# Spreading the loads of a fused attention and gMLP kernel between its compute, and moving the copies of V next to their use

## The chip, the cores and the metric

One core of one Trainium2 chip. The metric is the device time of one execution in microseconds (us), the median of several. Five engines matter: PE (matmuls; PEld is its weight load), DVE (vector), ACT (activation), POOL (here it issues the loads, and does some small arithmetic), and SP, which issues the stores. Each engine works through its own queue of instructions in order, as the stall shown below makes visible for DVE. The granted clock is the share of its full clock that PE was allowed to run at, as the profile records it. All executions quoted here are fast: none was more than 1.5% slower than the fastest of the same kernel.

## The reference

Eight batches of 576 positions, eight heads of 64. Heads 0 to 3 attend to the last 32 positions ("plain"), heads 4 to 7 to every fourth of the last 128 ("dilated"). The result is x of a gated MLP whose gate mixes positions with the 576 x 576 matrix w_sg.

```python
attn = softmax(where(mask, q @ k.T / 8, -1e9)) @ v        # per batch and head
x    = attn as [8, 576, 512]
h    = gelu(x @ w_in);  u, v2 = halves of h
v_n  = (v2 - mean) / sqrt(var + 1e-6) * g_ln              # over the 512 columns
out  = x + (u * (w_sg @ v_n + b_sg)) @ w_out
```

## The kernel before

The kernel runs ten periods p. In period p the attention of batch p is done, z and u of batch p-1, and the gate and output of batch p-2. Each period has two halves: transposes T and scores S with gate and output, then AV and the transposes X with z and u. Operations stay in program order on each engine. The parts that the change touches:

```python
def load(b, step):                       # all loads of a batch, issued by POOL
    ...                                  # q, k, v of the plain heads, q, k of the dilated
    x = v[b][4:8].rearrange("h (m r) d -> m h (r d)", r=4)
    dma(vm.rearrange("p h r d -> p h (r d)"), x[0:KB])
    for r in range(2):
        dma(vt[r:KB:2]..., x[NM - 64:NM, :, D * r:D * r + 3 * D])
    nc.vector.tensor_copy(vd[:, :, 0:4, 0:D], vm)                  # DVE, waits for vm
    nc.vector.tensor_copy(vd[:, :, 4:6, 0:D], vt[:, :, 0:3:2, :])  # DVE, waits for vt

def a_T(b, g):                           # q and k transposed by PE, then copied
    ...
    nc.scalar.copy(k0, pk[0:64, :, 0:HS])            # ACT
    nc.vector.tensor_copy(k1, pk[64:128, :, 0:HS])   # DVE: needed before the scores

setup_consts(); load(0, 2); load_weights(); load(1, 4)
for p in range(B + 2):
    merge(T and S of p, gate and output of p - 2)    # period 0: also prep_wsg
    merge(AV and X of p, z and u of p - 1)
    if p + 2 < B:
        load(p + 2, 4)                   # behind all compute of the period
```

The masks of heads 3 and 7, and the two small operations rs (a power of the variance), are done by POOL, in the same queue as the load issues.

The softmax here doesn't subtract the row's maximum and nothing guards it: scores larger than these inputs give would overflow.

## Time and profile before

| | before |
|---|---|
| median | 417.7 us |
| busy: PE / DVE / ACT / POOL | 61% / 46% / 44% / 34% |
| length of periods 2 to 6 | 47.4 to 48.9 us |
| DVE idle ahead of the vm copies | 127.6 us over 8 copies |
| granted PE clock, whole span | 0.88 |

No engine is near full. These are the engine line of the profile page, and its strip of 40 slices of about 10.5 us: a digit is the busy share in tenths, or the granted clock in tenths.

```profile
PE 256.0 (61%) x2494; PEld 180.3 (43%) x2494; DVE 191.5 (46%) x378; ACT 183.2 (44%) x270; POOL 140.3 (34%) x193
...
PE   1010285198518972598808974378807978889994
...
DVE  7000472248035560638317380556407386486280
...
PEclk9999999998958987598956988599865999989999
```

DVE drops to 0 or near it again and again, and the clock digit of PE drops to 5 or 6 about as often. The list of waits says who waited for whom (total us, times, longest):

```profile
DVE vd_90 L151 <- DMA vm<-in_v_dram: 72.4, 4, 24.7
DVE vd_89 L151 <- DMA vm<-in_v_dram: 55.2, 4, 15.4
```

Its PE part shows the wait that follows from that one:

```profile
PE pss L214 <- DVE kT_1_83 L205: 24.1, 2, 12.7
PE pss L214 <- DVE kT_1_79 L205: 22.8, 2, 11.6
PE pss L214 <- DVE kT_1_81 L205: 22.7, 2, 12.0
PE pw L167 <- DMA wsg_73<-in_moe_w_sg_dram: 21.2, 1, 21.2
...
PE pxt L270 <- DVE onorm L254: 16.6, 12, 2.1
```

The timeline shows one such stall (start, duration, engine, line, operation; in brackets the idle time before it and what ended it):

```profile
150.44 3.14 POOL L121 DMA_DIRECT2D qp<-in_q_dram  x4
...
152.57 0.96 DVE L254 TENSOR_TENSOR onorm<-poa,rc 128x768 f16<-128x768 f32 x1
...
156.13 1.39 PE L336 MATMUL pv<-wsgT_74,vn 128*128 128x288 f16 x10 [0.15 <-ACT xT L279]
...
160.74 1.30 POOL L121 DMA_DIRECT2D vt<-in_v_dram  x2
168.91 0.43 DVE L151 COPY vd_89<-vm 128x1024 f16<-128x1024 f16 x1 [15.37 <-DMA vm<-in_v_dram]
170.04 0.29 DVE L152 COPY vd_89<-vt 128x512 f16<-128x512 f16 x1 [0.71 <-DMA vt<-in_v_dram]
170.37 0.76 DVE L205 CAST kT_1_79<-pk 64x576 f16<-64x576 f32 x1
...
171.18 0.64 PE L214 MATMUL pss<-qT,kT_0_78 128*128 128x96 f16 x6 [11.24 <-DVE kT_1_79 L205]
...
173.31 2.56 PE L336 MATMUL pv<-wsgT_74,vn 128*128 128x288 f16 x10 [0.64 <-DVE kT_1_81 L205]
```

POOL starts to issue the loads only when period 2's compute has left its queue, at 150.4, and needs until 162.0. The last of them lands at 170.0. DVE finished its work of the period at 153.5, but the next thing in its queue is the copy of vm, which belongs to batch 4 and will not be read before the second half of period 4. Behind it stands the kT copy that period 3's scores need at once. Thus DVE waits 15.4 us, and PE 11.2 us. Ten L336 matmuls take 1.39 us before the stall and 2.56 us after it.

### The profile page before, as it was taken

What the parts mean: (1) busy time and instruction counts of PE and PEld (TensorE: products, weight loads), DVE (VectorE), ACT (ScalarE), POOL (GpSimd) and SP (SyncE); (2) the same over time, 40 slices, a digit from 0 to 9 for tenths busy, and PEclk for the clock granted to TensorE, in tenths of its full rate; (3) what the DMA queues carried; (4) which work ended last, traced back from release to release, by engine and by line L of the source; (5) the groups of instructions that cost most, each with busy time, mean ns of one, the idle gap of its engine ahead of it and who ended that gap; (6) DMA issues with size and microseconds to landing.
All of it is one profiled execution on the core that took longest, in us unless ns stands there. A gap on an engine that the chain in (4) does not pass through costs nothing.

```text
span 418.0 us, 6143 instructions
## 1 busy us (share of the span) xinstructions
PE 256.0 (61%) x2494; PEld 180.3 (43%) x2494; DVE 191.5 (46%) x378; ACT 183.2 (44%) x270; POOL 140.3 (34%) x193
## 2 busy tenths in 40 slices
PE   1010285198518972598808974378807978889994
PEld 0010184165415551454605653255605557556462
DVE  7000472248035560638317380556407386486280
ACT  2000076074613853256803755157713768564422
POOL 8736039025801275013911167013920220130030
PEclk9999999998958987598956988599865999989999
DMA  9999509701960369111990339411990300110303
GB/s 129 140 205 115 73 2 103 94 2 7 106 83 0 114 45 134 17 54 62 82 112 2 115 20 121 55 52 63 63 133 3 114 2 2 72 44 0 114 0 113
DMA packets 91467, 28.91 MB, mean 69 GB/s; under 512 B 71664, under 2 KB 86064, under 8 KB 91440
## 3 DMA queue, kind: packets, MB, share of 16 engines
q0 software_dynamic: 85232, 18.47, 49.9%
q1 hardware_dynamic: 6208, 10.06, 7.0%
q8 instruction: 19, 0.31, 0.3%
q14 instruction: 8, 0.07, 0.0%
HBM read 37.53 MB, written 9.44 MB: 112 GB/s over the span
## 4 chain that ended last, share of the span: by engine, by line
PE 22%; DVE 22%; DMA 19%; POOL 18%; ACT 12%; issue 6%; POOLq 0%; ACTq 0%; DVEq 0%
DMA vt<-in_v_dram 14%; PE po L353 6%; DVE st L303 5%; PE pv L336 5%; DMA w_out_72<-in_moe_w_out_dram 4%; POOL kp L121 4%; DVE vs L340 3%; PE pu L323 3%; POOL qp L121 3%; ACT osb L359 3%; DVE gat L343 2%; DVE onorm L254 2%; ACT vv L298 2%; PE po L356 2%; POOL vp_88 L121 2%
## 5 line engine op out<-in xcount | busy, mean ns | idle before, releaser
L336 PE MATMUL pv<-wsgT_74,vn 128*128 128x288 f16 x320 | 52.2, 320 | 8.6 <-ACT qT L196 2.9
L196 ACT CAST qT<-pq 128x576 f16<-128x576 f32 x32 | 20.6, 644 | 65.2 <-PE pq L185 49.6
L353 PE MATMUL po<-w_out_72,gat 128*128 128x512 f16 x160 | 42.7, 379 | 10.4 <-DVE gat L343 8.5
L323 PE MATMUL pu<-xT,w_in_71 128*128 128x288 f16 x256 | 43.8, 326 | 2.0 <-ACT xT L279 1.9
L336 PEld LDWEIGHTS <-vn 128*128 128x128 f16 x320 | 34.4, 108 | 22.3 <-issue 9.9
L294 PE MATMUL pz<-w_in_71,xT 128*128 128x512 f16 x160 | 39.0, 394 | 0.0
L359 ACT COPY osb<-po 128x1024 f32<-128x1024 f32 (+1 forms) x24 | 21.0, 875 | 39.9 <-PE po L356 32.5
L303 DVE BATCH_NORM_STATS2 st<-vv 128x6 f32<-128x512 f32 x40 | 26.9, 673 | 21.5 <-ACT vv L298 21.4
L151 DVE COPY vd_90<-vm 128x1024 f16<-128x1024 f16 x4 | 1.7, 429 | 72.4 <-DMA vm<-in_v_dram 72.4
L323 PEld LDWEIGHTS <-w_in_71 128*128 128x128 f16 x256 | 26.7, 110 | 11.1 <-issue 2.5
L254 DVE TENSOR_TENSOR onorm<-poa,rc 96x768 f16<-96x768 f32 (+1 forms) x32 | 30.6, 955 | 1.1
L340 DVE SCALAR_TENSOR_TENSOR vs<-pv,g_col,b_bc 128x576 f16<-128x576 f32 x32 | 26.1, 816 | 8.7 <-PE pv L336 8.1
L326 ACT ACTIVATE u<-pu 128x576 f16<-128x576 f32 x32 | 22.2, 693 | 17.5 <-PE pu L323 17.5
L151 DVE COPY vd_89<-vm 128x1024 f16<-128x1024 f16 x4 | 1.7, 429 | 55.2 <-DMA vm<-in_v_dram 55.2
L167 PE MATMUL pw<-ident_69,wsg_73 96*128 96x96 f16 x30 | 2.9, 277 | 39.2 <-DMA wsg_73<-in_moe_w_sg_dram 21.2
L121 POOL DMA_DIRECT2D qp<-in_q_dram x32 | 25.3, 797 | 3.7 <-DMA kd<-in_k_dram 2.0
L121 POOL DMA_DIRECT2D kp<-in_k_dram x32 | 23.1, 735 | 9.2 <-DMA w_in_71<-in_moe_w_in_dram 4.3
L305 POOL TENSOR_SCALAR rs<-mv 128x2 f32<-128x2 f32 (+1 forms) x24 | 5.8, 240 | 60.2 <-DVE mv L304 60.2
L270 PE MATMUL pxt<-ident_69,onorm 96*128 96x96 f16 (+2 forms) x192 | 15.3, 221 | 16.8 <-DVE onorm L254 16.6
L298 ACT ACTIVATE vv<-pz 128x1024 f32<-128x1024 f32 (+1 forms) x24 | 21.0, 881 | 8.6 <-PE pz L294 7.8
L353 PEld LDWEIGHTS <-gat 128*128 128x128 f16 x160 | 14.0, 97 | 23.7 <-DVE gat L343 13.0
L294 PEld LDWEIGHTS <-xT 128*128 128x128 f16 x160 | 15.3, 102 | 16.9 <-issue 2.7
(179 smaller groups left out, 552.4 us busy)
## 6 DMA issues: line engine op xcount, KB each, us to landing
out_dram<-osb SPq DMA_DIRECT2D x32, 256.0 KB, 2.2
qp<-in_q_dram POOLq DMA_DIRECT2D x32, 72.0 KB, 3.0
kp<-in_k_dram POOLq DMA_DIRECT2D x32, 72.0 KB, 3.1
qd<-in_q_dram POOLq DMA_DIRECT2D x8, 288.0 KB, 7.5
kd<-in_k_dram POOLq DMA_DIRECT2D x8, 288.0 KB, 8.5
vm<-in_v_dram POOLq DMA_DIRECT2D x8, 256.0 KB, 8.8
vt<-in_v_dram POOLq DMA_DIRECT2D x16, 96.0 KB, 8.6
vp_88<-in_v_dram POOLq DMA_DIRECT2D x4, 288.0 KB, 6.0
```

What stands on the lines that cost most here:

```text
L121: nc.gpsimd.dma_start(dst, src)
L196: nc.scalar.copy(qT, pq[:, :, 0:HS])
L254: nc.vector.tensor_tensor(onorm.rearrange("p a h d -> p h a d"), pv[:, :, :, 0:64], rc.unsqueeze(3).broadcast_to([rows, 2, NB, 64]), AO.mult)
L294: nc.tensor.matmul(pz[:, c, :], xT[:, g4, MT[ti]:MT[ti] + 128], w_in16[:, g4, DH:DFF], start=(g4 == 0), stop=(g4 == 3))
L298: nc.scalar.activation(vv[:, 0:n], pz[:, 0:n], AF.Gelu_apprx_tanh)
L303: nc.vector.bn_stats(st[:, c, :], vv[:, c, :])
L323: nc.tensor.matmul(pu[:, j, 0:HS], w_in16[:, g4, 128 * ph:128 * ph + 128], xT[:, g4, HS * j:HS * j + HS], start=(g4 == 0), stop=(g4 == 3))
L326: nc.scalar.activation(us[b][:, ph, :].rearrange("p (j w) -> p j w", j=2), pu[:, :, 0:HS], AF.Gelu_apprx_tanh)
L336: nc.tensor.matmul(pv[:, j, 0:HS], vn[:, kp, 128 * ph:128 * ph + 128], wsgT16[:, kp, HS * j:HS * j + HS], start=(kp == 0), stop=(kp == 4))
L340: nc.vector.scalar_tensor_tensor(vs.rearrange("p (j w) -> p j w", j=2), pv[:, :, 0:HS], g_col[:, ph:ph + 1], b_bc.rearrange("p (j w) -> p ...
L353: nc.tensor.matmul(po[:, c, :], gat[:, ph, ts], w_out16[:, ph, :], start=(ph == 0), stop=False)
L359: nc.scalar.copy(osb[:, 0:n], po[:, 0:n])
```

## The change

Its intent: get the loads off the critical path, by splitting a batch's loads into pieces, putting the pieces between compute one to two periods ahead of use, moving the vd copies to the period that reads them, and moving the w_sg transposes from period 0 to 1. A new merge rule comes with it, for three lists in place of two. The core of the diff (comments stand for what is cut):

```diff
-        nc.vector.tensor_copy(vd[:, :, 0:4, 0:D], vm)              # inside load(b)
-        nc.vector.tensor_copy(vd[:, :, 4:6, 0:D], vt[:, :, 0:3:2, :])
+    def cp_vd(b):                                   # now a piece of its own
+        vm, vt = vraw.pop(b)
+        vd = vds[b % NV]
+        nc.vector.tensor_copy(vd[:, :, 0:4, 0:D], vm)
+        nc.vector.tensor_copy(vd[:, :, 4:6, 0:D], vt[:, :, 0:3:2, :])
...
-    def merge(one, other):                          # i1 * n2 <= i2 * n1 decides whose turn it is
+    def merge(*lists):
+        items = [((i + 0.5) / len(x), n, i, f) for n, x in enumerate(lists)
+                 for i, f in enumerate(x)]
+        for _, _, _, (f, *a) in sorted(items, key=lambda t: t[:3]):
+            f(*a)
...
-    load(0, 2); load_weights(); load(1, 4)
+    # batch 0 and w_in here; batch 1 inside period 0, w_sg at its end, w_out in period 1
     for p in range(B + 2):
-                   (a_S, p, 6), (a_S, p, 7)]
-        if p == 0:
-            mlp = [(prep_wsg,)]
+                   (a_S, p, 6), (a_S, p, 7), (cp_vd, p)]
+        if p == 1:
+            mlp = [(prep_wsg, i) for i in range(5)]
+        # first half:  io = [(ld_vp, p + 1, 0, 4), (ld_vd, p + 1)]
+        # second half: io = [(ld_plain, p + 2, 0), (ld_plain, p + 2, 2), (ld_dil, p + 2)]
-        if p + 2 < B:
-            load(p + 2, 4)
```

More of the change, by code (lines that the diff above doesn't have):

```diff
@@ L117, in setup_consts @@
             nc.vector.memset(t[:, S:PTW], 1.0)
+        nc.vector.memset(wsgT16[0:64, 4, :], 0.0)
     def dma(dst, src):
@@ L123, with open_batch @@
     loaded = {}
-    def load(b, step):
+    def open_batch(b):
         qp = ld.tile([QB, NB, 4, D], FP16, tag="qp", name="qp")
@@ L129, in load, with ld_plain, ld_dil, ld_vp @@
         kd = ld.tile([TB, 4, 2, 4, D], FP16, tag="kd", name="kd")
+        loaded[b] = ((qp, kp), (qd, kd))
+    def ld_plain(b, h0):
+        if h0 == 0:
+            open_batch(b)
+        for t, src in zip(loaded[b][0], (q, k)):
+            for h in range(h0, h0 + 2):
+                dma(t[:, :, h, :], src[b][h].rearrange("(a p) d -> p a d", p=QB))
+    def ld_dil(b):
+        for t, src in zip(loaded[b][1], (q, k)):
+            dma(t.rearrange("p h f r d -> p (h f) (r d)"),
+                src[b][4:8].rearrange("h (f p r) d -> p (h f) (r d)", p=TB, r=4))
+    def ld_vp(b, h0, n):
+        vp = vps[b % NV]
+        x = v[b][h0:h0 + n].rearrange("h (a p) d -> p (h a) d", p=QB)
+        y = vp[:, h0:h0 + n].rearrange("p h a d -> p (h a) d")
+        dma(y[HALO:KB, :, 0:D], x)
+        dma(y[0:HALO, 1:, 0:D], x[QB - HALO:QB, 0:n * NB - 1])
+    vraw = {}
+    def ld_vd(b):
         vm = ld.tile([KB, 4, 4, D], FP16, tag="vm", name="vm")
         vt = ld.tile([KB, 4, 3, D], FP16, tag="vt", name="vt")
-        vp, vd = vps[b % NV], vds[b % NV]
-        loaded[b] = ((qp, kp), (qd, kd), vp, vd)
-        for h0 in range(0, 4, step):
-            hs = slice(h0, h0 + step)
-            for t, src in ((qp, q), (kp, k)):
-                for h in range(h0, h0 + step):
-                    dma(t[:, :, h, :], src[b][h].rearrange("(a p) d -> p a d", p=QB))
-            x = v[b][hs].rearrange("h (a p) d -> p (h a) d", p=QB)
-            y = vp[:, hs].rearrange("p h a d -> p (h a) d")
-            dma(y[HALO:KB, :, 0:D], x)
-            dma(y[0:HALO, 1:, 0:D], x[QB - HALO:QB, 0:step * NB - 1])
-        for t, src in ((qd, q), (kd, k)):
-            dma(t.rearrange("p h f r d -> p (h f) (r d)"),
-                src[b][4:8].rearrange("h (f p r) d -> p (h f) (r d)", p=TB, r=4))
         x = v[b][4:8].rearrange("h (m r) d -> m h (r d)", r=4)
@@ L150, in load, with ld_win, ld_wsg @@
                 x[NM - 64:NM, :, D * r:D * r + 3 * D])
+        vraw[b] = (vm, vt)
+    def cp_vd(b):
+        vm, vt = vraw.pop(b)
+        vd = vds[b % NV]
         nc.vector.tensor_copy(vd[:, :, 0:4, 0:D], vm)
         nc.vector.tensor_copy(vd[:, :, 4:6, 0:D], vt[:, :, 0:3:2, :])
-    def load_weights():
+    def ld_win():
         dma(w_in16, moe_w_in.rearrange("(g p) f -> p g f", p=128))
+    def ld_wsg():
+        dma(wsg16, moe_w_sg.rearrange("(a p) s -> p a s", p=QB))
         nc.sync.dma_start(b_bc, moe_b_sg.unsqueeze(0).to_broadcast([128, S]))
@@ L158, in load_weights, with ld_wout, prep_wsg @@
             nc.sync.dma_start(g_col, moe_g_ln.rearrange("(c p) -> p c", p=128))
-        dma(wsg16, moe_w_sg.rearrange("(a p) s -> p a s", p=QB))
+    def ld_wout():
         dma(w_out16, moe_w_out.rearrange("(g p) f -> p g f", p=128))
-    def prep_wsg():
-        nc.vector.memset(wsgT16[0:64, 4, :], 0.0)
-        for kp in range(5):
-            pw = psum("pw")
-            for a in range(NB):
-                nc.tensor.matmul(
-                    pw[:, a // 3, QB * (a % 3):QB * (a % 3) + QB],
-                    wsg16[:, a, MT[kp]:MT[kp] + 128], ident16[0:QB, 0:QB],
-                    start=True, stop=True)
-            lo = 64 if kp == 4 else 0
-            nc.vector.tensor_copy(
-                wsgT16[lo:128, kp, :].rearrange("p (j w) -> p j w", j=2),
-                pw[lo:128, :, 0:HS])
+    def prep_wsg(kp):
+        pw = psum("pw")
+        for a in range(NB):
+            nc.tensor.matmul(
+                pw[:, a // 3, QB * (a % 3):QB * (a % 3) + QB],
+                wsg16[:, a, MT[kp]:MT[kp] + 128], ident16[0:QB, 0:QB],
+                start=True, stop=True)
+        lo = 64 if kp == 4 else 0
+        nc.vector.tensor_copy(
+            wsgT16[lo:128, kp, :].rearrange("p (j w) -> p j w", j=2),
+            pw[lo:128, :, 0:HS])
     qkT, PTs, onorms, xTs = {}, {}, {}, {}
     def a_T(b, g):
-        plain, dil, _, _ = loaded[b]
+        plain, dil = loaded[b]
         pq, pk = psum("pq"), psum("pk")
@@ L234, in a_AV @@
     def a_AV(b, g):
-        _, _, vp, vd = loaded[b]
+        vp, vd = vps[b % NV], vds[b % NV]
         poa = psum("poa")
@@ L362, in m_out @@
             nc.sync.dma_start(out[b][MT[ti] + lo:MT[ti] + 128, :], osb[lo:128, c, :])
-    def merge(one, other):
-        n1, n2 = len(one), len(other)
-        i1 = i2 = 0
-        while i1 < n1 or i2 < n2:
-            if i2 >= n2 or (i1 < n1 and i1 * n2 <= i2 * n1):
-                f, *a = one[i1]
-                i1 += 1
-            else:
-                f, *a = other[i2]
-                i2 += 1
+    def merge(*lists):
+        items = [((i + 0.5) / len(x), n, i, f) for n, x in enumerate(lists)
+                 for i, f in enumerate(x)]
+        for _, _, _, (f, *a) in sorted(items, key=lambda t: t[:3]):
             f(*a)
     setup_consts()
-    load(0, 2)
-    load_weights()
-    load(1, 4)
+    for h0 in (0, 2):
+        ld_plain(0, h0)
+    ld_vp(0, 0, 4)
+    ld_dil(0)
+    ld_vd(0)
+    ld_win()
     for p in range(B + 2):
-        att, mlp = [], []
+        att, mlp, io = [], [], []
         if p < B:
@@ L393 @@
                    [(m_out, p - 2, i) for i in range(3)])
-        merge(att, mlp)
-        att, mlp = [], []
+        if p + 1 < B:
+            if p == 0:
+                io = [(ld_plain, 1, 0), (ld_plain, 1, 2), (ld_dil, 1)]
+            io += [(ld_vp, p + 1, 0, 4), (ld_vd, p + 1)]
+        if p == 0:
+            io += [(ld_wsg,)]
+        if p == 1:
+            io += [(ld_wout,)]
+        merge(att, mlp, io)
+        att, mlp, io = [], [], []
         if p < B:
@@ L402 @@
             mlp += [(m_zu, p - 1, ph) for ph in range(1, 4)]
-        merge(att, mlp)
         if p + 2 < B:
-            load(p + 2, 4)
+            io = [(ld_plain, p + 2, 0), (ld_plain, p + 2, 2), (ld_dil, p + 2)]
+        merge(att, mlp, io)
 _INS = ['q', 'k', 'v', 'moe_w_in', 'moe_g_ln', 'moe_w_sg', 'moe_b_sg', 'moe_w_out']
```

## The prediction

> **What bounds the kernel now.** No engine is full: the page's busy shares are PE 61%, DVE 46%, ACT 44%, POOL 34%. The loads bound it. In the chain of waits "DMA vt<-in_v_dram" alone holds 14% of the span. The mechanism, from the timeline of one period: the loads of batch p+2 are queued on POOL after all compute of period p; POOL issues them from 150.4 to 162.0 us, the last landing at 170.0. The two vd copies stand in DVE's in-order queue ahead of the next period's first kT copy, so DVE sits idle 15.4 us (list of waits: 72.4 + 55.2 us over 8 such copies), and PE, needing kT, idles 11.2 us. This repeats six times at a period of 48.2 us, and batch 1 delays period 0 in the same way (24.7 us).
>
> A second cost follows: after each idle stretch PE is slow. The windows view gives granted clock 0.50 to 0.62 in the first 7.8 us, and ten L336 matmuls take 2.5 us there, 1.39 us elsewhere. The Trainium skill, "TensorE: Matmul & The Clock Gate" (Part 1), says that an idle window of about 3.4 us halves the clock until sustained work restores it; the trace agrees.
>
> **What the change does.** It removes no work. Copies of vd move to the end of the first half of the period that uses them, a period after their loads were issued; loads are issued between compute, a period or more before use. Added on POOL: nothing, but its 15 load issues (about 0.8 us each, 12 us a period) now stand between the masks and the rs operations, which can be late by up to 3 us. w_sg's transposes (PE 2.9, DVE 3.5 us) move from period 0 to 1. The new merge order should fill PE gaps of 2.1 (before X1) and 1.8 us (before the output).
>
> **Size.** Period 7 in the present trace has no load stall either before or after it: PE runs from 346.5 to 380.7, 34.2 us, at clock 0.97. With vd copies (+0.7 us), some POOL lateness, and 1 to 3 us from better interleaving I estimate 33.3 us for periods 2 to 7: 200 us. The tail (380.7 to the end) is unchanged: 37 us. Start: batch 0 lands by 22 us, w_in by 27, batch 1 by about 43, w_sg by about 46. Period 1 stops at its first w_sg transpose until then, and lasts some 27.5 us after it: 73.5 us, against 122 now. Sum 73.5 + 200 + 37 = 311; I add 2 for contention of load issue with DVE.
>
> Predicted 313 us, 80% range 299 to 334. Faster by over 2%: 0.98; within: 0.015; slower: 0.005.
>
> **What would show each step.** DVE's waits on vm and vt vanish after the start; no PE idle over 4 us in periods 2 to 7; periods 32 to 35.5 us apart; granted clock there at least 0.9; PE busy falls to about 225 us from 256 with the same count; one remaining long PE wait, on w_sg, at about 40 to 46 us.
>
> **What would make it wrong.** POOL as the new in-order bottleneck: an issue waits for the load eight before it (seen at the start: kp waits on w_in), and the mask of head 3 or 7 or rs waits behind it. DVE operations slowing POOL's descriptor writing: "SBUF — State Buffer" (SBUF: two separate sides) tells of such a lock; issues beside busy DVE took 0.79 against 0.73 us, so small here. Transfers of 20 us per batch plus output may crowd a 33 us period. Then 320 to 335.

## The result, and the profile after

The median is 318.5 us (317.7 to 319.0) against 417.7 us (416.2 to 420.5). The ratio is 0.762, 95% interval 0.757 to 0.766. A ratio here is the mean time of one kernel's fast runs over that of the other's in the same rounds, so it is not quite the ratio of the medians. The profile page, with slices of about 7.9 us:

```profile
PE 233.4 (74%) x2494; PEld 164.5 (52%) x2494; DVE 200.2 (63%) x378; ACT 185.3 (59%) x270; POOL 140.7 (44%) x191
...
PE   0373548868877779768876979768877878788984
...
DVE  7533339957669493949478393949488665961760
...
PEclk9999999979999999999999899999999999999999
```

DVE no longer drops to 0 before the last slice, and the clock digit is 9 almost throughout. PE does the same 2494 matmuls in 23 us less. DVE's 378 operations take 9 us more, which the prediction did not expect: nearly all of it lies in the eight vt copies (6.4 us) and the gate products gat (3.2 us), and experiment 9 tells why. The list of waits has no DVE entry for vm or vt at all. The largest PE waits in it:

```profile
PE pxt L288 <- DVE onorm L272: 32.3, 23, 1.9
...
PE po L371 <- DVE gat L361: 8.6, 8, 1.1
...
PE poa L265 <- POOL PT_94 L249: 5.0, 1, 5.0
...
PE pw L185 <- DMA wsg_73<-in_moe_w_sg_dram: 4.8, 1, 4.8
```

(Line numbers moved: L151 is now L167, L205 is L223, L254 is L272, L270 is L288.) The long waits of before are gone. In their place stand many short ones, above all for onorm before the X transposes: 32.3 us, against 16.6 us before. The timeline of one period, cut to what matters:

```profile
88.67 1.89 PE L312 MATMUL pz<-w_in_71,xT 128*128 128x512 f16 x8
...
89.21 0.42 DVE L167 COPY vd_89<-vm 128x1024 f16<-128x1024 f16 x1
...
89.43 1.33 POOL L249 TENSOR_TENSOR PT_94<-PT_94,masks 128x576 f16<-128x576 f16 x1 [6.61 <-ACT PT_94 L246]
89.54 1.37 DVE L168 COPY vd_89<-vt 128x512 f16<-128x512 f16 x1
...
93.02 0.66 DVE L321 BATCH_NORM_STATS2 st<-vv 128x6 f32<-128x512 f32 x1
...
94.19 0.95 DVE L272 TENSOR_TENSOR onorm<-poa,rc 96x768 f16<-96x768 f32 x1
...
95.20 0.43 PE L288 MATMUL pxt<-ident_69,onorm 96*128 96x96 f16 x6 [1.86 <-DVE onorm L272]
...
105.33 0.42 PE L203 MATMUL pq<-ident_69,qp 96*128 96x96 f16 x6
```

The copies now find their data there: no idle time stands before them. The vt copy takes 1.37 us where it took 0.29 us before; it started 0.1 us after POOL's mask and ended 0.15 us after it.

Taken from the first q transpose of a period to that of the next, periods 2 to 6 take 35.0 us on average, (245.28 - 70.33) / 5. Period 7 runs from 245.28 to the first gate product of period 8 at 279.37, 34.1 us. The span of 316.6 us is 70.3 us up to period 2, 209.0 us for periods 2 to 7, and 37.3 us of tail.

### The profile page after: what moved, and what is told of

The parts are those of the page before. It is cut to its first block, busy times and chain, and to the rows that moved or that the text cites. A ratio compares the mean times of both kernels' runs of the same rounds, so it can differ in the third digit from the quotient of the medians.

```text
span 316.6 us, 6153 instructions
## 1 busy us (share of the span) xinstructions
PE 233.4 (74%) x2494; PEld 164.5 (52%) x2494; DVE 200.2 (63%) x378; ACT 185.3 (59%) x270; POOL 140.7 (44%) x191
## 4 chain that ended last, share of the span: by engine, by line
DVE 35%; PE 29%; POOL 13%; ACT 10%; DMA 7%; issue 5%; POOLq 0%; DVEq 0%; ACTq 0%
PE po L371 10%; DVE st L321 7%; DVE vs L358 6%; DVE onorm L272 5%; DVE gat L361 5%; PE pz L312 4%; DMA w_in_71<-in_moe_w_in_dram 4%; POOL kp L122 3%; PE pv L354 3%; PE po L374 3%; DVE vn L331 3%; DMA wsg_73<-in_moe_w_sg_dram 3%; ACT vv L316 3%; POOL rs L324 3%; POOL qp L122 2%
## 5 line engine op out<-in xcount | busy, mean ns | idle before, releaser
L371 PE MATMUL po<-w_out_72,gat 128*128 128x512 f16 x160 | 42.7, 379 | 8.6 <-DVE gat L361 8.6
L354 PE MATMUL pv<-wsgT_74,vn 128*128 128x288 f16 x320 | 43.9, 286 | 5.4 <-DVE kI_86 L223 1.2
L288 PE MATMUL pxt<-ident_69,onorm 96*128 96x96 f16 (+2 forms) x192 | 15.3, 220 | 32.8 <-DVE onorm L272 32.3
L354 PEld LDWEIGHTS <-vn 128*128 128x128 f16 x320 | 30.8, 97 | 14.6 <-issue 5.6
L312 PE MATMUL pz<-w_in_71,xT 128*128 128x512 f16 x160 | 38.1, 379 | 0.2 <-ACT PT_95 L246 0.2
L341 PE MATMUL pu<-xT,w_in_71 128*128 128x288 f16 x256 | 37.9, 295 | 0.0
L321 DVE BATCH_NORM_STATS2 st<-vv 128x6 f32<-128x512 f32 x40 | 27.0, 675 | 16.0 <-ACT vv L316 16.0
L323 POOL TENSOR_SCALAR rs<-mv 128x2 f32<-128x2 f32 (+1 forms) x24 | 6.8, 282 | 59.9 <-DVE mv L322 59.5
L288 PEld LDWEIGHTS <-onorm 96*128 96x128 f16 (+1 forms) x192 | 10.6, 104 | 40.3 <-DVE onorm L272 40.3
L272 DVE TENSOR_TENSOR onorm<-poa,rc 96x768 f16<-96x768 f32 (+1 forms) x32 | 30.6, 956 | 1.1
L295 ACT CAST xT<-pxt 128x512 f16<-128x512 f32 x16 | 20.8, 1300 | 17.3 <-PE pxt L288 17.2
L341 PEld LDWEIGHTS <-w_in_71 128*128 128x128 f16 x256 | 23.9, 100 | 6.0
L331 DVE TENSOR_SCALAR vn<-vv,mv,rs 128x512 f16<-128x512 f32 x40 | 21.3, 570 | 2.8 <-POOL rs L324 2.8
L312 PEld LDWEIGHTS <-xT 128*128 128x128 f16 x160 | 14.6, 98 | 14.0 <-issue 0.3
```

Source lines behind the costliest of these rows:

```text
L272: nc.vector.tensor_tensor(onorm.rearrange("p a h d -> p h a d"), pv[:, :, :, 0:64], rc.unsqueeze(3).broadcast_to([rows, 2, NB, 64]), AO.mult)
L288: nc.tensor.matmul(pxt[:, s // 3, c:c + n], onorm[:, s, :, :], ident16[0:rows, 0:n], start=True, stop=True)
L312: nc.tensor.matmul(pz[:, c, :], xT[:, g4, MT[ti]:MT[ti] + 128], w_in16[:, g4, DH:DFF], start=(g4 == 0), stop=(g4 == 3))
L321: nc.vector.bn_stats(st[:, c, :], vv[:, c, :])
L331: nc.vector.tensor_scalar(vn[:, ti, :], vv[:, c, :], mv[:, c, 0:1], rs[:, c, :], AO.subtract, AO.mult)
L341: nc.tensor.matmul(pu[:, j, 0:HS], w_in16[:, g4, 128 * ph:128 * ph + 128], xT[:, g4, HS * j:HS * j + HS], start=(g4 == 0), stop=(g4 == 3))
```

## The experiments

Two theories stood against each other. Theory A: what cost the time is the place of two copies in DVE's in-order queue, and any move of them that puts them behind more urgent work gives the whole gain. Rival B: the loads are issued too late and in too large a block, and spreading them is what pays. Further questions: what the slow PE clock cost, what the w_sg move and the new order are worth, and whether POOL has become a brake.

All ratios are to the kernel before, run on the same chip in the same rounds. Each kernel gave the right result.

| kernel | median us | ratio (95%) |
|---|---|---|
| changed kernel | 318.5 | 0.762 (0.757 to 0.766) |
| 1: before, only the copies moved | 311.6 | 0.745 (0.742 to 0.749) |
| 2: changed, copies back behind their loads | 326.0 | 0.780 (0.777 to 0.784) |
| 3: changed, w_sg in period 0 | 325.1 | 0.777 (0.774 to 0.780) |
| 4: changed, old order | 306.8 | 0.733 (0.730 to 0.737) |
| 5: before, PE kept busy in the stall | 417.3 | 0.994 (0.990 to 0.999) |
| 8: as 1, w_sg in period 1 | 308.5 | 0.735 (0.732 to 0.739) |
| 9: as 4, all masks on DVE | 303.3 | 0.724 (0.721 to 0.728) |
| 10: as 4, loads behind the last rs | 304.9 | 0.728 (0.724 to 0.732) |
| 11: changed, old order in second halves | 310.7 | 0.741 (0.737 to 0.746) |
| 12: 4, 9 and 10 together, w_sg transposed later | 296.2 | 0.706 (0.703 to 0.709) |

### 1: the copies alone

```diff
 # in the kernel before
-        nc.vector.tensor_copy(vd[:, :, 0:4, 0:D], vm)
-        nc.vector.tensor_copy(vd[:, :, 4:6, 0:D], vt[:, :, 0:3:2, :])
+        vraw[b] = (vm, vt)          # copied by cp_vd(b)
...
-                   (a_S, p, 6), (a_S, p, 7)]
+                   (a_S, p, 6), (a_S, p, 7), (cp_vd, p)]
```

> The kernel before with one thing moved: the two vd copies of a batch go from behind its loads to the end of the first half of the period that uses them. Loads stay in one block after the compute, w_sg stays in period 0, the old merge order stays. Theory A (DVE's in-order queue, blocked by copies that wait for a load, is the whole loss): 312 to 328 us, DVE's waits on vm and vt gone, periods of 34 to 36 us. Rival B (the loads themselves come too late or in too large a block, so splitting and interleaving them is what pays): 370 us or more, with PE or POOL waiting for loads in place of DVE.

Measured: 311.6 us, ratio 0.745, just below theory A's range. Moving two copies gives all of the gain, and more than the whole change: its interval lies wholly below the changed kernel's. Its list of waits has no vm or vt on DVE. What it still has is the start of before:

```profile
PE pw L174 <- DMA wsg<-in_moe_w_sg_dram: 21.4, 1, 21.4
```

Its periods 2 to 6 take 32.4 to 33.1 us, shorter than the changed kernel's and than the 34 to 36 us that I expected. So theory A holds as a sufficient cause, and something in the change costs time.

### 2: the early loads, with the copies right behind them

```diff
 # in the changed kernel, ld_vd(b)
         vraw[b] = (vm, vt)
+        cp_vd(b)
...
-                   (a_S, p, 6), (a_S, p, 7), (cp_vd, p)]
+                   (a_S, p, 6), (a_S, p, 7)]
```

> The changed kernel with the vd copies put back directly behind their loads, everything else (split and interleaved loads, one period earlier, w_sg in period 1, new order) kept. Theory A: DVE again stands still for each batch, now only from the middle of the first half for issue plus landing, some 5 to 8 us a period, so 345 to 370 us. Rival B: within 2% of the changed kernel, 313 to 325 us.

Measured: 326.0 us. Neither range held it, and theory A's was the worse miss. The DVE waits on loads that remain:

```profile
DVE vd L168 <- DMA vm<-in_v_dram: 21.1, 3, 10.8
DVE vd L169 <- DMA vt<-in_v_dram: 4.0, 6, 0.8
```

There are three waits for vm instead of eight; the two long ones, 10.1 and 10.8 us, lie before period 2. Period 2 starts at 77.0 us instead of 70.3, and the periods from there take 35.1 us on average, (252.67 - 77.00) / 5, against 35.0. So 6.7 of the 7.2 us between the two spans are lost before period 2. In the later periods the copies cost hardly anything although they stand right behind their loads: the loads are now issued in the middle of other work, and by the time DVE's queue reaches the copy the data has landed or nearly so. The stall therefore had two sufficient cures. A copy must not stand in the queue ahead of urgent work before its data is due; one may move the copy back or the load forward. Doing both gives the gain once. The run does not part the two wholly: the copies follow their loads to the end of the first half, so they too stand elsewhere in DVE's queue. Early loads with the copies still ahead of the next period's kT copy were not run.

### 3: w_sg in period 0

```diff
 # in the changed kernel
     ld_win()
+    ld_wsg()
...
-        if p == 1:
+        if p == 0:
             mlp = [(prep_wsg, i) for i in range(5)]
-        if p == 0:
-            io += [(ld_wsg,)]
```

> The changed kernel with w_sg loaded right behind w_in and transposed in period 0, as before. If the later transposition of w_sg has a real share in the gain: 328 us or more. My theory, that it only trades a PE wait of 5 us in period 1 for one in period 0: 315 to 325 us, with one long PE wait on w_sg until about 29 us.

Measured: 325.1 us, just above what I expected (315 to 325). Later transposition is worth 0.777 - 0.762 = 0.015 of 417.7 us, some 6 us, and not nothing. PE's wait for w_sg is 20.2 us here (4.8 us in the changed kernel), and period 2 starts at 76.4 us instead of 70.3.

### 4 and 11: the order

```diff
 # in the changed kernel
-        merge(att, mlp, io)
+        merge_old(att, mlp, io)   # att and mlp by the old rule, then io spread over the result as before
```

Experiment 4 does this in both halves of each period, experiment 11 in the second half alone.

> The changed kernel, with attention and MLP work of each half merged by the old rule; the pieces of loads are spread as in the changed kernel. The prediction's claim that the new order gains 1 to 3 us a period: 324 to 336 us. Rival, from the changed kernel's trace, where PE waits 32.3 us for onorm before the X transposes against 16.6 before, and its periods without loads still take 34.1 us: the order is worth nothing or costs, 308 to 321 us.

> The changed kernel with the old merge rule in the second half of each period only (output products, z and X transposes); the first half keeps the new rule. If the whole loss of the new order lies in the second half, where PE waits for onorm before the X transposes: 305 to 310 us, like the run with the old order in both halves (306.8). If it lies in the first half: 315 to 320 us, as the changed kernel.

Measured: 306.8 us with the old order in both halves, 310.7 us in the second half only. The first lies below even the rival's range (308 to 321 us). The new order costs 0.762 - 0.733 = 0.029 of 417.7 us, 12 us, where the prediction booked a gain. Of this 0.762 - 0.741 = 0.021 (9 us) comes back from the second half; the rest is the first half's (the intervals of 4 and 11 just touch), so the cause is probably not in one place, and the 310.7 us lie just above the range expected of the second half alone. Periods 2 to 6 take 32.9 us in experiment 4, (234.44 - 69.77) / 5, against 35.0. PE's waits in 70 to 280 us of both spans agree. The changed kernel:

```profile
PE pxt L288 <- DVE onorm L272: 27.1, 18, 1.9
```

Experiment 4:

```profile
PE pxt L288 <- DVE onorm L272: 16.2, 12, 1.9
```

All of PE's idle time in periods 2 to 7 is 42.7 us in the changed kernel and 29.3 us in experiment 4, a difference of the size of the loss. Of the two gaps that the prediction wanted to fill, the new order closes the one before X1 (1.94 us in experiment 4, 0.07 us in the changed kernel) and not the one before the output (1.1 us in both). It opens three others: 1.9 us before X0, 1.0 to 1.3 us before X2, and 1.1 to 1.6 us before X3 in every period, where experiment 4 has 0 to 1.6 us (about 0.5 in three of six).

The old rule issues AV of heads 0 and 1 before the first z product, so DVE makes the first onorm while PE works on z, and the first X (X0) can follow. A stretch of experiment 4's timeline shows it:

```profile
121.00 3.62 PE L312 MATMUL pz<-w_in,xT 128*128 128x512 f16 x16
...
121.35 1.37 DVE L168 COPY vd<-vt 128x512 f16<-128x512 f16 x1
...
123.01 0.95 DVE L272 TENSOR_TENSOR onorm<-poa,rc 96x768 f16<-96x768 f32 x1
...
124.00 0.69 DVE L321 BATCH_NORM_STATS2 st<-vv 128x6 f32<-128x512 f32 x1
...
124.98 0.42 PE L288 MATMUL pxt<-ident,onorm 96*128 96x96 f16 x6
```

The first onorm is ready at 123.96, and X0 starts at 124.98 without any wait. In the changed kernel's timeline above, z comes first, DVE is given its statistics (L321) before onorm, and PE waits 1.86 us. That the statistics ahead of onorm are the reason was read from the timelines; no run moved them alone.

### 5: what the slow clock cost

```diff
 # in the kernel before, m_sgu, behind the products
+        if ph == 1 and b <= 4:
+            for _ in range(100):
+                nc.tensor.matmul(pv[:, 1, HS:512], ident16, w_in16[:, 0, 0:512 - HS],
+                                 start=True, stop=True)
```

> The kernel before, unchanged but for 100 matmuls that nobody reads, put behind the second w_sg product of periods 2 to 6, where PE otherwise stands still for 11 us. It prices the slow PE clock after the stall, apart from the stall. If the slow clock adds time of its own (the first stretch after a stall took 10.5 us from kT copy to the last gate product, against 8.9 us in period 7 with a warm PE): granted clock after the stalls near 1.0 and some 2 us less in each of 5 periods, 404 to 411 us. Rival, the slow clock is hidden behind DVE: 416 to 420 us. If the added matmuls outlast the stall they cost time and the run says nothing.

Measured: 417.3 us against 419.4 us for the kernel before in the same rounds; ratio 0.994, a gain of 0.1% to 1%, and 2 us in the middle. That is in the rival's range and not in that of the slow clock (404 to 411 us). The windows view of 8 us after a stall gives, after the length, busy us of PE, PEld, DVE, ACT and POOL, then the granted clock. The kernel before:

```profile
170.30:178.30 8.00, 6.27 (x49) 4.61 (x49) 6.62 (x12) 3.14 (x5) 0.00 (x0) 0.50 0.00 0
218.50:226.50 8.00, 6.01 (x48) 4.46 (x48) 6.61 (x12) 2.91 (x5) 0.00 (x0) 0.50 0.01 3
```

Experiment 5:

```profile
170.00:178.00 8.00, 5.11 (x58) 3.66 (x57) 7.04 (x12) 3.15 (x5) 1.27 (x1) 1.00 0.00 0
218.00:226.00 8.00, 6.16 (x56) 4.24 (x55) 6.19 (x10) 2.49 (x4) 1.27 (x1) 0.81 0.00 0
```

In these two windows the clock was 1.00 and 0.81 instead of 0.50; after the other three stalls it was 0.79, 0.82 and 0.62, so the clock was mended only in part. In the one period where it was full, ten L336 matmuls took 1.39 us again, and that period took 46.2 us against 48.2 in the kernel before. The other four were between 0.8 us shorter and 0.8 us longer than before. So the run shows that a partly mended clock gains little. What a full clock in every period would gain was not shown; from that single period my estimate is up to 2 us each, 10 us in all, against the 99 us that the change gains. That the slow clock was mainly a companion of the stall fits the lengths: before, a period of 48.2 us less DVE's idle 16.1 us (15.4 and 0.7) leaves 32.1 us, and experiment 1, in the old order without the stall, takes 32.4 to 33.1 us, although its vt copies take longer (1.37 us in place of 0.29).

### 8: do spread loads add anything?

```diff
 # experiment 1, and:
-    load(0, 2); load_weights(); load(1, 4)
+    load(0, 2); w_in, b_sg, g_ln; load(1, 4); w_sg, w_out
...
-        if p == 0:
-            mlp = [(prep_wsg,)]
+        if p == 1:
+            mlp = [(prep_wsg, [i]) for i in range(5)]
```

> The first experiment (copies moved, loads of a batch still in one block behind the compute, old order) with w_sg loaded behind batch 1 and transposed in period 1. If splitting the loads and spreading them between the compute gains anything once the copies are moved, this stays above the run with old order and spread loads (306.8 us), by 2% or more: 313 us or above. My theory, that spreading adds nothing more: 302 to 308 us.

Measured: 308.5 us, ratio 0.735; my range ended at 308. It differs from experiment 4 (0.733), which has the same order, the same copies and w_sg in the same period, in that its loads are still one block behind the compute. The intervals overlap, so splitting and spreading the loads adds nothing that these runs can show once the copies are out of the way. The changed kernel and its parts thus add up, in steps of the ratio times 417.7 us:

| step | ratio | us |
|---|---|---|
| copies moved (1) | 1.000 to 0.745 | -106 |
| w_sg one period later (8) | 0.745 to 0.735 | -4 |
| loads split and spread (4) | 0.735 to 0.733 | -1, not clear of noise |
| new merge order (changed kernel) | 0.733 to 0.762 | +12 |

Each of the first and third steps depends on the order in which they are taken, as experiment 2 shows.

### 9 and 10: POOL

```diff
 # 9: experiment 4, and
-        eng = nc.gpsimd if h % 4 == 3 else nc.vector
+        eng = nc.vector
 # 10: experiment 4, and the second half's q and k loads start at 0.36 of it, behind the last rs
-        merge_old(att, mlp, io)
+        merge_old(att, mlp, io, 0.36)
```

> The changed kernel in the old order, with the masks of heads 3 and 7 on DVE in place of POOL. At the start the mask of head 3 stood behind 20 load issues (PE waited 5 us for it), and a POOL mask seems to hold up DVE operations (a vt copy took 1.37 us beside one, 0.29 alone). If both hold: 297 to 304 us, the copy at 0.29 us again. If POOL's help is worth its price, DVE's added 0.46 us twice a period makes it 308 us or more.

> The changed kernel in the old order, with the q and k loads of the second half issued behind the last rs of the period instead of four of them ahead of it. If POOL's lateness costs what the prediction feared (about 0.5 us a period by DVE's wait of 0.47 us on rs): 301 to 305 us and DVE's wait on rs gone. Rival, it is hidden: 305 to 308 us.

Measured: 303.3 us for 9 and 304.9 us for 10, each within its first range, though the interval of 10 (0.724 to 0.732) overlaps that of 4 (0.730 to 0.737): a gain of 2 us is likely and not proved. In 10, DVE's wait on rs falls from 2.8 us in six waits to 0.5 us in one, as expected. In 9, DVE takes over 16 masks of 0.46 us, 7.3 us of work, and its busy time still falls from 199.0 to 195.6 us. Two groups of its list of groups tell why (busy us, mean ns):

```profile
L361 DVE TENSOR_TENSOR gat<-u,vs 128x576 f16<-128x576 f16 x32 | 14.7, 458 | 1.7
...
L168 DVE COPY vd<-vt 128x512 f16<-128x512 f16 x8 | 2.3, 286 | 0.0
```

The same groups of experiment 4, which differs only in having these masks on POOL:

```profile
L361 DVE TENSOR_TENSOR gat<-u,vs 128x576 f16<-128x576 f16 x32 | 17.7, 553 | 1.7
...
L168 DVE COPY vd<-vt 128x512 f16<-128x512 f16 x8 | 8.8, 1096 | 0.0
```

The Trainium skill, "SBUF — State Buffer" (Who interferes with whom), says that POOL and DVE share one pair of ports as an exclusive lock, and that a DVE copy in a two-port mode, or a DVE operation with two SBUF inputs (against a POOL operation that reads SBUF, as a mask does), has to wait while a POOL operation holds it. The runs agree: the vt copy takes 1.10 us on average with the masks on POOL and 0.29 us without, the gat product 0.55 and 0.46 us. In experiment 4 only six of the eight copies and six of the 32 products overlap a mask in time, and these take 1.37 and 0.96 us; every other product takes 0.46 us. POOL's help with a mask of 0.46 us cost DVE more than it saved.

### 12: what the runs point to

```diff
 # the old order, masks on DVE, loads behind the last rs, and
-        if p == 1:
-            mlp = [(prep_wsg, i) for i in range(5)]
+        if p == 1:
+            att += [(prep_wsg, i) for i in range(5)]    # behind S and the vd copies of period 1
```

> All that the runs point to: the changed kernel in the old order, masks of heads 3 and 7 on DVE, second-half loads behind the last rs, and the w_sg transposes at the end of period 1's first half, so that PE has that half to work on while w_sg lands (it waited 10.6 us for it with the masks on DVE). If these add up: 303.3 us less 2 for the rs less up to 9 of the wait on w_sg, 292 to 297 us. If they hide each other: 300 to 303 us.

Measured: 296.2 us, ratio 0.706, within the first range, and 7% less than the changed kernel, (0.762 - 0.706) / 0.762. Its profile page begins:

```profile
PE 236.1 (80%) x2494; PEld 168.5 (57%) x2494; DVE 196.1 (67%) x394; ACT 183.3 (62%) x270; POOL 118.0 (40%) x175
```

Period 2 starts at 62.3 us instead of 70.3. It is the fastest kernel of this study.

## Why the prediction was right or wrong

The time was within the range, and 5.5 us (2%) above the value. Point by point:

- **The load stall as the bound, by way of DVE's queue: right, and shown.** Experiment 1 takes away this alone and gains 106 us. DVE's waits on vm and vt vanish in the changed kernel.
- **"A second cost follows: after each idle stretch PE is slow": the observation was right, the cost small as far as it was shown.** The clock (0.50 to 0.66 over the first 7.8 us after each stall of periods 2 to 6) came back to 0.99, as said, but mending it in part gains some 2 us (experiment 5). It was no term of the sum, so it did not spoil the number.
- **The start, 73.5 us:** measured 70.3. PE's wait on w_sg came about where it was said, ending at 43.7 us, and was 4.8 us long. The mask of head 3 behind the load issues cost another 5.0 us of PE's time, which the prediction named only as a risk.
- **"1 to 3 us from better interleaving", 33.3 us a period: this step failed.** Periods 2 to 7 took 209.0 us and not 200; they lay 34.1 to 36.0 us apart, one of them outside the 32 to 35.5 us named. The new order costs 12 us (experiment 4), 2.1 us a period where 1 to 3 us of gain were booked: it fills one of the two gaps that I had seen and opens three ahead of X0, X2 and X3.
- **Period 7 as the measure of an unstalled period, 34.2 us: only half right.** Experiment 4's period 7, with its vd copies, takes 33.1 us (234.44 to 267.52) where the prediction reckoned 34.2 + 0.7. The slow clock is not the reason: both have the same granted clock (0.95; the 0.97 of the prediction is not what the windows view gives) and the same PE busy time (28.6 us), so the difference is PE's waits. A baseline some 2 us too long and a gain that was a loss of 2 us cancelled in part.
- **The sum:** against its parts, periods 2 to 7 cost 9.0 us more, the start 3.2 us less, the tail 0.3 us more, the 2 us booked for contention are not found as a cost of their own, and 1.9 us of the device time lie outside the profiled span, which the sum left out. That the value was only 5.5 us off is partly luck.
- **The tail, 37 us:** measured 37.3.
- **Contention, 2 us:** the direction looked at, DVE slowing POOL's load issues, does not show. The prediction's 0.79 and 0.73 us are those of q and of k issues: in the changed kernel a q issue takes 0.80 us both beside a busy DVE (28 issues) and beside an idle one (4), a k issue 0.73 us in both cases (16 and 10). The other direction, POOL's masks slowing DVE, was not foreseen and is larger. Experiment 9 gains 0.733 - 0.724 = 0.009, 4 us, though it also lets the mask of head 3 start at once in period 0: of the 3.2 us between the two spans, 0.9 us are gained before period 2.
- **PE busy 225 us:** measured 233.4; the direction was right, the size too hopeful.
- **No PE idle time over 4 us in periods 2 to 7:** right; the longest is 1.9 us.
- **Rival B, that spreading the loads pays:** the prediction did not part the two. They are two cures of one stall, as far as experiment 2 parts them; given the moved copies, spreading adds nothing that shows.

## What to carry to other kernels

Where an engine works in order, look at what stands at the head of its queue during a stall, and ask when that is needed: here a 0.43 us copy, needed some one and a half periods later, held up everything behind it. Move that one instruction first and measure, before restructuring all loads; and when a change comes with a new order of the work, measure the order alone, because it can quietly take back a tenth of the gain. A small job handed to a second engine that shares a port with the first can cost the first more than the job.

## What the Trainium skill lacked or had wrong

- "TensorE: Matmul & The Clock Gate" (HAM oscillation) warns of PE idle gaps above some 3.4 us. The halved clock was there (0.50 to 0.66 over the first 7.8 us after each stall), but mending it in part gained at most 1% (0.994, 0.990 to 0.999), probably because another engine was waited for. The page does not say to check that first. A gap of that length was not needed, either: in experiment 4, PE was busy for 1.47 us of the stretch from 93.4 to 96.8 us, with no gap over 1.94 us, and the granted clock of the next 3.4 us was 0.51. It also says (Part 1) that about 3.4 us of sustained work restores the clock; here 6.0 to 6.3 us of PE work within 8 us did not, perhaps because it was not sustained.
- "SBUF — State Buffer" gives most room to DVE starving POOL's load issues. Here nothing of it shows (a q issue takes 0.80 us beside a busy DVE and beside an idle one); the other direction, a POOL mask of 1.3 us stretching a DVE copy of 0.29 us to 1.37 us, was worth more. The page's rule covers it, and gives no time for operations this short.
- No page shows what a single wait for a load, placed too early in an in-order compute queue, can cost: here DVE stood still for 15.4 us a period, in six periods.
- No page mentions what the start shows on POOL: an issue waits until the load eight issues earlier has landed (3.9 us for w_in in the changed kernel). The trace shows this as a wait in the program: the loads use eight semaphores in turn, and each issue waits for its own semaphore. No limit of the chip is shown by it.
